# Where twelve weight sums run, when four prologue steps come, and one load that no longer waits: a Fourier filter followed by a gated MLP on one core

## The chip, the core and the metric

The kernel runs on one core of a Trainium2 chip. A core has TensorE (PE, matrix products, with its weight loads shown as PEld), VectorE (DVE), ScalarE (ACT), GpSimd (POOL) and SyncE (SP, which here only issues transfers). Each engine executes its own instructions in order; semaphores tie the engines together. Transfers issued by SP and ACT go to two queues of their own, those issued by POOL to a third. The metric is the device time of one execution in microseconds (us), the median of several.

## The reference

```python
def _attn_ref(x, filt_r, filt_i):               # x: (8, 3008, 256)
    X = np.fft.rfft(x, axis=1)
    Y = X * (filt_r + 1j * filt_i)[None, :, :]  # one complex filter, 1505 x 256
    return np.fft.irfft(Y, n=x.shape[1], axis=1).astype(np.float32)

def _moe_ref(x, w_in, w_out):                   # x: (24064, 256), w_in: 256 x 2048
    h = x @ w_in
    return ((h - np.tanh(h)) @ w_out).astype(np.float32)   # w_out: 2048 x 256
```

The second function takes the output of the first, its eight sequences laid one after the other. The weights arrive as 64-bit floats and are turned into 32-bit floats by integer operations on VectorE.

## The kernel before

**The two halves.** A sequence of 3008 is split as 64 times 47. "There" and "back" (the transforms of length 64 and 47, as products with constant matrices) turn a sequence into its spectrum and out again, with a multiplication by the filter between them. The back half ends in tiles `ut` of tokens; each group of up to four residues (256 or 224 tokens a column block) goes through the up product (256 to 2048), the shrink `h - tanh(h)`, and the down product (2048 to 256). There are 48 groups (8 sequences, 6 groups each); a group is worked in four units, and the running number of a unit is `U` (0 to 191). In unit `U` the program writes out the up product of `U`, the shrink of `U - 1` and the down product of `U - 2`.

**Products with seven instead of eight blocks.** From `U = 4` on, up and down are done with a Strassen-Winograd scheme: seven block products (`up` L564, `down` L707) instead of eight. It needs sums of the weight blocks, made once by `sums(u)` (L220): four additions of 128x256 for each of the eight weight quarters, 0 to 3 of `w_in` (tile `wu`), 4 to 7 of `w_out` (tile `wd`). It also needs sums of the tokens (`tu`) and of the shrunk values (`t`), made by `combine` (L557) on VectorE as long as weights are pending, on GpSimd later. One sum is written over a plain block, so `sums(u)` may come only after the last plain use of that quarter (`up_plain` L636, `down_plain` L788, used for `U` under 4).

**The prologue.** Sequence 0 has nothing to hide behind. It is filtered in seven slots `g` (0 to 6): `across` (transposes), `forth` (products and L377, L378), `filtered` (L389 to L401, on VectorE, with one addition, L398, on GpSimd for the slots 0 to 4), and `back0` (L1039, products L1048 and L1050, copies L1053 on ScalarE, stores to `ct2` L1054). A slot's way back is written out one slot later, so that its products follow those of the next slot's way there. The filter tiles are loaded by `filters_of` (L1021 to L1032), from slot 2 on by SP. The last slot needs one filter row that is turned round, with its sign changed: `turned_rows` (L488) loads it into `neg`, in its second step multiplies it by -1 on VectorE (L501), stores it as `less` (L502) and copies it from there into `filt` (L492), from which SP loads the last slot's tile (L1028) and seven further pieces (L1031). The two stores and the copy are issued by POOL, and the copy waits for the store's landing.

At the end of the prologue the first token tile `e2` is read back from `ct2` (`rest`, L1034, twice: first slots 0 to 4, then 5 and 6). Meanwhile TensorE runs four steps for sequence 1 (L1136) and 14 filler products (`warmer`, L999).

**Weights.** Sixteen pieces of weights are converted. The last eleven are taken by the generator `weights` (L238): it issues the loads (L169) on POOL, and each call of `next` gives one step. Its argument `after` names the quarters whose sums follow the conversion of a piece. Inside a unit, `e()` takes up to three steps and `t(k)` two of them, five times a unit each.

**What fills the gaps.** Between the blocks of a unit `t(k)` places steps of the transforms for later sequences: the first products of sequence 1 (`first`, L266, products L295, copies L297) are placed at the positions in `due`, in units of `5 U + k`.

**Order.** Everything here is in the order in which it is written; no planner moves instructions. An instruction late on VectorE therefore delays all that is behind it there. PSUM tiles of the main part have one buffer each: a product that reuses `x`, `y`, `z` or `t` waits until the last reader has taken the old contents out (for the `z` bank that is L618 or L634, for `y` L601, for `x` L626; the token products `pu`, L537, and the first products L295 share the banks `t` and `y`).

Of the kernel before, what the change touches and what calls it, by code (L numbers as in the profile page):

```python
# [9 lines left out]
F32 = mybir.dt.float32  # L10
# [17 lines left out]
NX = NH // XH  # L28
# [10 lines left out]
LEAD = 34  # L39
# [72 lines left out]
def kernel(  # L112
# [10 lines left out]
    V, G, ACT = nc.vector, nc.gpsimd, nc.scalar  # L123
# [14 lines left out]
    cst = ctx.enter_context(tc.tile_pool(name="cst", bufs=1))  # L138
# [10 lines left out]
    def extent(g):  # L149

        n = SLOTS[g][1] * NH
        return (n, DM) if g < len(SLOTS) - 1 else (2 * n, DM // 2)
# [67 lines left out]
    def sums(u):  # L220

        w = (wu if u < 4 else wd)[:, :, 256 * (u % 4):256 * (u % 4) + 256]
        by = G if 4 <= u < 7 else V
        by.tensor_add(w[:, 4], w[:, 6], w[:, 3])
        yield
        for to, one_in, less in ((5, 4, 0), (2, 1, 5), (6, 0, 6)):
            by.tensor_sub(w[:, to], w[:, one_in], w[:, less])
            yield

    def begun(tiles, job, queue=nc.sync):  # L230
# [150 lines left out]
    def filtered(g, xy, ft, by, by2, pool=None):  # L381

        n, w = extent(g)
        ab = xy.rearrange("p (x v) c -> p x v c", v=2)
        ft = ft[0:n, :, 0:w]
        fv = ft.rearrange("p (x v) c -> p x v c", v=2)
        nn = (tr.tile([128, 4, DM], F32, tag="nn", bufs=1, name="nn") if pool is None else
              pool.tile([KM, 4, DM], F32, tag="nn", bufs=3, name="nn"))[0:n, :, 0:w]
        by.tensor_mul(nn.rearrange("p (x v) c -> p x v c", v=2), ab,  # L389
                      fv[:, :, 0:1].to_broadcast([n, 2, 2, w]))  # L390
        yield nn
        if pool is not None:
            fi = ft[:, 1:4:2]
            V.tensor_mul(xy[:, 1:3], xy[:, 1:3], fi)
            V.tensor_sub(nn[:, 0:4:3], nn[:, 0:4:3], xy[:, 1:3])
            V.tensor_mul(xy[:, 0:4:3], xy[:, 0:4:3], fi)
            yield
            by2.tensor_add(nn[:, 1:3], nn[:, 1:3], xy[:, 0:4:3])  # L398
            yield
            V.tensor_add(xy[:, 0:2], nn[:, 0:2], nn[:, 2:4])  # L400
            V.tensor_sub(xy[:, 2:4], nn[:, 0:2], nn[:, 2:4])  # L401
            yield
            return
        by.tensor_mul(ab, ab, fv[:, :, 1:2].to_broadcast([n, 2, 2, w]))
        yield
        by2.tensor_sub(nn[:, 0:4:3], nn[:, 0:4:3], xy[:, 1:3])
        by2.tensor_add(nn[:, 1:3], nn[:, 1:3], xy[:, 0:4:3])
        yield
        V.tensor_add(xy[:, 0:2], nn[:, 0:2], nn[:, 2:4])
        V.tensor_sub(xy[:, 2:4], nn[:, 0:2], nn[:, 2:4])  # L410
        yield
# [97 lines left out]
    def load_e2(b, c, parts=None, tiles=None):  # L509

        e2, gt = tiles or (tr.tile([128, CH, DM], F32, tag="e2", bufs=2, name="e2"),
                           tr.tile([128, CH, 64], F32, tag="gt", bufs=2, name="gt"))
        if tiles is None:
            nc.sync.dma_start(gt, (pairs_d if b else g_d)[:, CH * 64 * c:CH * 64 * (c + 1)])
        if parts is None:
            nc.sync.dma_start(e2, dram(ct2[b], CH * c * DM,
                                       [[(PAD if b else NH) * DM, 128], [1, CH * DM]]))
        return e2, gt
# [5 lines left out]
    e2s, uts = {}, {}  # L524
# [38 lines left out]
    hs, gs = {}, {}  # L563

    def up(U, d, e, s, t):

        i, u = divmod(U, 4)
# [382 lines left out]
    with tc.tile_pool(name="tr", bufs=2) as tr, tc.manual_schedule():  # L950
# [16 lines left out]
        with tc.tile_pool(name="pro", bufs=1) as pro, \  # L967
# [55 lines left out]
            def filters_of(g):  # L1023

                t, queue = filt[g % 3], G if g < 2 else nc.sync
                if g == len(SLOTS) - 1:
                    V.memset(t[0:1, 2:4], 0.0)
                    queue.dma_start(t[NH:KL, 2:4], dram(filt_d, (turned * 8 + 5) * DM,  # L1028
                                                        [[8 * DM, NH], [2 * DM, 2], [1, DM]]))
                for v, row, n, src in filter_rows(g):  # L1030
                    queue.dma_start(t[row:row + n, v], src)  # L1031
                return t  # L1032
# [73 lines left out]
            fts = {0: filters_of(0)}  # L1106
# [42 lines left out]
            last_g = len(SLOTS) - 1  # L1149
# [19 lines left out]
            for g in range(last_g + 1):  # L1169
                if g + 2 <= last_g:  # L1170
                    fts[g + 2] = filters_of(g + 2)
                    a2[g + 2] = across(g + 2)
                if g == 3:
                    e2s[0] = load_e2(0, 0, ())
                    ones_1 = first1(load_x(big([128, 8, DM], F32, "x1"), 1, 0, 8))
                if g == last_g - 1:
                    under(fts[last_g])
                    convert(3)
                    way_back()
                if g < last_g:  # L1180
                    there[g + 1] = there0(g + 1)
                next(there[g][0])
                if g < last_g - 1:
                    convert(3)
                xy = there.pop(g)[1]
                chain = filtered(g, xy, fts.pop(g), V, V if g >= last_g - 1 else G, pro)
                nn = next(chain)
                for _ in range(2):
                    next(chain)
                if g in summed:  # L1190
                    next(chain)
                ended.append((back, (0, g, xy, z0, (ACT, nc.sync))) if g in summed else (back0, (g, nn)))
                if g not in (0, last_g - 1):
                    way_back()
                if g == 1:
                    next(turning)
                if g == 2:
                    ahead = [begun(tiles1, job, queue=G) for job in jobs[5:7]]
            rest(0, SG * (last_g - 1), [nc.sync])
            way_back()  # L1200
            rest(SG * (last_g - 1), NA - SG * (last_g - 1), [nc.sync])
            there_yet = cst.tile([128, 1], F32, name="there_yet")
            G.tensor_copy(there_yet, e2s[0][0][:, 0, 0:1])
            fs = first(2, z2, [(1, c) for c in range(2, NX)])
            next(fs)
            convert(100)
            late = weights(tiles1, jobs[5:], G, ahead, 3,
                           after={6: (0,), 8: (1,), 10: (2, 3, 4, 5, 6)})
            next(late)
            for _ in ones_1:  # L1210
                pass
# [2 lines left out]
        with tc.tile_pool(name="dn", bufs=2) as dn, \  # L1214
# [60 lines left out]
                                 start=True, stop=True)  # L1275
            for _ in range(4):
                next(late)
            due = [7 + (LEAD - 7) * k / (NX + 4) for k in range(NX + 4)]
            plan = []
            kinds = {(2, 0): "there", (1, 3): "back"}  # L1280
            kinds.update({at: "filter" for at in FILTERED})
# [2 lines left out]
            for U in range(total + 2):  # L1284
                i, u = divmod(U, 4)
                if U == 6:
                    assert not pending
                    late = sums(7)
                if U == 3:
                    G.dma_start(mats[:, 0:10 * PAD], wide_d[0:KM])  # L1290
                if U < total:
# [18 lines left out]
                def converting(n):  # L1310

                    for _ in range(n):
                        if next(late, pending) is pending:
                            pending.clear()
# [5 lines left out]
                def e():  # L1320

                    next(dw, None)
                    converting(3 if U > 1 else 1)

                def s():

# [85 lines left out]
```

## Time and profile before

| | us |
|---|---|
| median of 3 executions (2583.92 to 2587.75) | 2584.98 |
| the profiled execution | 2587.2 |
| its span | 2585.3 |
| TensorE busy in it | 2556.4 (99%) |
| VectorE busy | 1821.1 (70%) |
| ScalarE busy | 1661.8 (64%) |
| GpSimd busy | 1475.9 (57%) |

The profiled execution took 2.2 us more than the median, and 1.9 us of it lie outside the span. TensorE is not idle more than 28.9 us in all. Its granted clock over the span is 0.996 of full speed. The columns of a window row are: the stretch, its length, the busy time and count of PE, PEld, DVE, ACT and POOL, then the granted clock of TensorE, the share of the transfer engines in use and GB/s. A timeline row has start, duration, engine, line, operation, output and inputs; in square brackets stands how long the engine had been idle before it and what released it. A row of the chain has start, length and the engine and line that the end of the program hung on at that time; its lengths run from one start to the next, so a row there is shorter than the pipelined duration of the same products in the timeline.

### The profile page before, as it was taken

What the parts mean: (1) busy time and instruction counts of PE and PEld (TensorE: products, weight loads), DVE (VectorE), ACT (ScalarE), POOL (GpSimd) and SP (SyncE); (2) the same over time, 40 slices, a digit from 0 to 9 for tenths busy, and PEclk for the clock granted to TensorE, in tenths of its full rate; (3) what the DMA queues carried; (4) which work ended last, traced back from release to release, by engine and by line L of the source; (5) the groups of instructions that cost most, each with busy time, mean ns of one, the idle gap of its engine ahead of it and who ended that gap; (6) DMA issues with size and microseconds to landing.
All of it is one profiled execution on the core that took longest, in us unless ns stands there. A gap on an engine that the chain in (4) does not pass through costs nothing.

```text
span 2585.3 us, 43442 instructions
## 1 busy us (share of the span) xinstructions
PE 2556.4 (99%) x16596; PEld 2176.2 (84%) x16596; DVE 1821.1 (70%) x2222; ACT 1661.8 (64%) x2482; POOL 1475.9 (57%) x1138
## 2 busy tenths in 40 slices
PE   8999999999999999999999999999999999999998
PEld 7668888888898888988888888888889888898887
DVE  6877776877567775778657876588766877555555
ACT  4556666666666666666666666666666666666665
POOL 5366665666556665665646565466655766545552
PEclk9999999999999999999999999999999999999999
DMA  8863216441434324333243432444231322110110
GB/s 222 265 178 105 70 30 123 111 102 44 95 75 106 86 59 93 84 88 94 50 101 80 102 78 51 94 96 103 66 71 42 93 66 43 33 32 18 25 21 18
DMA packets 345333, 214.30 MB, mean 83 GB/s; under 512 B 245337, under 2 KB 316535, under 8 KB 341469
## 3 DMA queue, kind: packets, MB, share of 16 engines
q1 hardware_dynamic: 321551, 170.82, 28.7%
q10 hardware_dynamic: 12142, 23.60, 3.0%
q0 software_dynamic: 11424, 17.03, 2.4%
q8 instruction: 132, 2.16, 0.3%
q14 instruction: 84, 0.69, 0.1%
HBM read 130.72 MB, written 83.39 MB: 83 GB/s over the span
## 4 chain that ended last, share of the span: by engine, by line
PE 96%; DVE 1%; DMA 1%; issue 0%; ACT 0%; POOL 0%; ACTq 0%; DVEq 0%; POOLq 0%
PE o L748 43%; PE x L578 25%; PE z L578 12%; PE y L578 6%; PE pm L360 2%; PE pu L537 2%; PE pf L307 1%; PE o L803 1%; PE pf L295 1%; PE o L648 0%; DMA fh<-f 0%; PE pm L362 0%; DMA neg<-in_filt_i_dram 0%; DMA mats_sb<-mats 0%; PE x L648 0%
## 5 line engine op out<-in xcount | busy, mean ns | idle before, releaser
L748 PE MATMUL o<-t,wd 128*128 128x256 f32 (+1 forms) x3008 | 762.1, 376 | 0.0
L558 POOL TENSOR_TENSOR t<-h 128x512 f32<-128x512 f32 (+1 forms) x186 | 305.3, 1641 | 740.1 <-DVE h L700 718.7
L700 DVE TENSOR_TENSOR h<-h,y 128x1024 f32<-128x1024 f32 (+1 forms) x384 | 577.3, 1503 | 165.4 <-ACT y L696 161.8
L748 PEld LDWEIGHTS o<-t,wd 128*128 128x128 f32 x3008 | 569.2, 190 | 82.4 <-POOL o L776 15.1
L578 PE MATMUL x<-tu,wu 128*128 128x256 f32 (+1 forms) x2256 | 579.0, 379 | 0.0
L748 PE MATMUL o<-h,wd 128*128 128x256 f32 (+1 forms) x2256 | 572.8, 376 | 1.8 <-DVE h L700 1.8
L584 ACT COPY s<-x 128x512 f32<-128x512 f32 (+1 forms) x188 | 108.8, 579 | 601.3 <-PE x L578 556.5
L748 PEld LDWEIGHTS o<-h,wd 128*128 128x128 f32 x2256 | 426.0, 190 | 71.4 <-issue 20.5
L578 PEld LDWEIGHTS x<-tu,wu 128*128 128x128 f32 x2256 | 420.9, 190 | 66.8 <-issue 13.5
L693 ACT ACTIVATE y<-y 128x1024 f32<-128x1024 f32 (+1 forms) x384 | 399.3, 1040 | 12.1
L696 ACT ACTIVATE y<-y 128x1024 f32<-128x1024 f32 (+1 forms) x384 | 399.8, 1041 | 4.6
L690 ACT ACTIVATE y<-h 128x1024 f32<-128x1024 f32 (+1 forms) x384 | 400.3, 1042 | 3.5 <-DVE h L626 1.7
L559 POOL TENSOR_TENSOR t<-h,t 128x512 f32<-128x512 f32 (+1 forms) x186 | 306.2, 1646 | 14.6
L560 POOL TENSOR_TENSOR t<-h 128x512 f32<-128x512 f32 (+1 forms) x186 | 288.4, 1551 | 0.0
L561 POOL TENSOR_TENSOR t<-h,t 128x512 f32<-128x512 f32 (+1 forms) x186 | 287.4, 1545 | 0.0
L584 ACT COPY u<-x 128x512 f32<-128x512 f32 (+1 forms) x376 | 213.7, 568 | 56.6 <-PE x L578 53.9
L626 DVE COPY h<-x 128x512 f32<-128x512 f32 (+1 forms) x188 | 127.9, 680 | 136.7 <-PE x L578 136.4
L578 PE MATMUL z<-ut,wu 128*128 128x256 f32 (+1 forms) x752 | 191.1, 377 | 3.6 <-DVE h L618 3.6
L578 PE MATMUL x<-ut,wu 128*128 128x256 f32 (+1 forms) x752 | 190.7, 376 | 0.0
L578 PE MATMUL y<-ut,wu 128*128 128x256 f32 (+1 forms) x752 | 190.0, 375 | 0.0
L578 PE MATMUL z<-tu,wu 128*128 128x256 f32 (+1 forms) x752 | 190.0, 375 | 0.0
L601 DVE TENSOR_TENSOR h<-y,s 128x512 f32<-128x512 f32 (+1 forms) x188 | 126.6, 673 | 69.6 <-PE y L578 62.3
(197 smaller groups left out, 2758.0 us busy)
## 6 DMA issues: line engine op xcount, KB each, us to landing
ft<-filt SPq DMA_DIRECT2D x28, 1024.0 KB
ct<-nn SPq DMA_DIRECT2D x56, 512.0 KB
e<-ct SPq DMA_DIRECT2D x47, 512.0 KB
a<-ct SPq DMA_DIRECT2D x112, 192.0 KB
out_dram<-ot SPq DMA_DIRECT2D x1248, 16.0 KB
x_sb<-in_x_dram SPq DMA_DIRECT2D x74, 256.0 KB
ct<-a ACTq DMA_DIRECT2D x62, 256.0 KB
gt<-g_pairs SPq DMA_DIRECT2D x42, 128.0 KB
```

Source lines behind the costliest of these rows:

```text
L558: by.tensor_sub(t[0], b[0][1], b[0][0])
L559: by.tensor_sub(t[1], b[1][1], t[0])
L560: by.tensor_sub(t[2], b[1][1], b[0][1])
L561: by.tensor_sub(t[3], b[1][0], t[1])
L578: nc.tensor.matmul(bank[:, k], wu[:, q - 1, (2 * u + k) * 128:(2 * u + k + 1) * 128], rhs[q - 1], start=(first and k == 0), stop=True, ski ...
L584: ACT.copy(t, X)
L626: V.tensor_copy(h[:, 2, :, 0:w], X)
L690: ACT.activation(y[k], ht[k], AF.Arctan, scale=TURN)
L693: ACT.activation(y[k], y[k], AF.Tanh, scale=BEND)
L696: ACT.activation(y[k], y[k], AF.Square, scale=SCALE, accum_out=y_sums[:, 2 * U + k // 2:2 * U + k // 2 + 1])
L700: V.tensor_mul(ht[k], ht[k], y[k])
L748: nc.tensor.matmul(product(q), wd[:, q - 1, (2 * u + k) * 128: (2 * u + k + 1) * 128], rhs[q - 1][:, k], start=(u == 0 and k == 0 and q == ...
```

## The change

- `sums` is done on VectorE for all eight quarters; before, the quarters 4, 5 and 6 were done on GpSimd.
- The generator takes only the quarters 2 and 4 behind the last piece of weights, and the quarters 3, 5, 6 and 7 are done from `U = 6` on (before: 2, 3, 4, 5 and 6 behind the last piece and 7 from `U = 6`). From `U = 6` on `e()` takes no step any more, so two steps follow each `t(k)`: ten in a unit.
- In slot 0 of the prologue the addition L398 is done by VectorE.
- The second step of the turned row (L501, L502, L492) is written behind slot 2, ahead of two loads of weights; before, it stood behind slot 1.
- The copy `there_yet` (L1203) is gone; POOL's loads of weights behind it no longer wait for the tile `e2`.
- `due` starts at position 4 instead of 7 and ends at the same place. One step of the first products moves into unit 0 for that, one other moves from right behind the token products of unit 3 to the end of that unit, and a later one (unit 8) falls away.

```diff
     def sums(u):
         w = (wu if u < 4 else wd)[:, :, 256 * (u % 4):256 * (u % 4) + 256]
-        by = G if 4 <= u < 7 else V
-        by.tensor_add(w[:, 4], w[:, 6], w[:, 3])
+        V.tensor_add(w[:, 4], w[:, 6], w[:, 3])
         yield
         for to, one_in, less in ((5, 4, 0), (2, 1, 5), (6, 0, 6)):
-            by.tensor_sub(w[:, to], w[:, one_in], w[:, less])
+            V.tensor_sub(w[:, to], w[:, one_in], w[:, less])
             yield
...
-                chain = filtered(g, xy, fts.pop(g), V, V if g >= last_g - 1 else G, pro)
+                chain = filtered(g, xy, fts.pop(g), V, V if g in (0, last_g - 1, last_g) else G, pro)
...
-                if g == 1:
+                if g == 2:
                     next(turning)
-                if g == 2:
                     ahead = [begun(tiles1, job, queue=G) for job in jobs[5:7]]
...
-            there_yet = cst.tile([128, 1], F32, name="there_yet")
-            G.tensor_copy(there_yet, e2s[0][0][:, 0, 0:1])
...
             late = weights(tiles1, jobs[5:], G, ahead, 3,
-                           after={6: (0,), 8: (1,), 10: (2, 3, 4, 5, 6)})
+                           after={6: (0,), 8: (1,), 10: (2, 4)})
...
-            due = [7 + (LEAD - 7) * k / (NX + 4) for k in range(NX + 4)]
+            due = [4 + (LEAD - 4) * k / (NX + 4) for k in range(NX + 4)]
...
                 if U == 6:
                     assert not pending
-                    late = sums(7)
+                    late = (None for u in (3, 5, 6, 7) for _ in sums(u))
...
                 def e():
                     next(dw, None)
-                    converting(3 if U > 1 else 1)
+                    converting((U < 6) * (3 if U > 1 else 1))
```

## The prediction, written before the changed kernel had run

> **What bounds the kernel now.** I read the page's first part, then the windows, then who waited for whom on TensorE, then the chain in order of time. The page says that TensorE is the bound and how little is left there.
>
> ```profile
> span 2585.3 us, 43442 instructions
> PE 2556.4 (99%) x16596; PEld 2176.2 (84%) x16596; DVE 1821.1 (70%) x2222; ACT 1661.8 (64%) x2482; POOL 1475.9 (57%) x1138
> ```
>
> 28.9 us are idle, and no matmul is removed. So the change can only win idle time and time at a slowed clock. The windows show where TensorE idles once the token products run:
>
> ```profile
> 128.00:137.00 9.00, 6.88 (x18) 4.24 (x18) 7.23 (x16) 3.62 (x7) 5.09 (x7) 0.81 0.85 220
> 137.00:157.00 20.00, 15.04 (x53) 9.98 (x52) 19.66 (x26) 8.40 (x13) 18.98 (x23) 0.95 0.77 213
> 187.00:205.00 18.00, 18.00 (x143) 15.66 (x142) 16.04 (x16) 12.27 (x18) 15.44 (x10) 1.00 0.22 50
> ```
>
> From 137 to 157 VectorE (third figure behind the length) is busy 19.66 of 20 us and GpSimd 18.98, TensorE 15.04: there VectorE is the bound. From 187 to 205 TensorE is full and VectorE has 2 us left. The waits of TensorE between 84 and 260 us, beside one in the chain:
>
> ```profile
> PE z L578 <- DVE h L618: 3.6, 1, 3.6
> PE pf L295 <- DVE h L601: 1.4, 1, 1.4
> ```
>
> ```profile
> 120.70 1.73 PE pf L295 x8
> ...
> 123.93 1.50 PE o L648 x4
> ...
> 128.25 2.10 issue
> 130.35 3.00 PE pf L295 x8
> 133.35 2.16 PE o L648 x4
> ...
> 155.16 2.08 PE z L578 x4
> 157.24 1.53 PE x L578 x4
> 158.77 0.86 PE y L578 x4
> ```
>
> Behind the waits of 2.1 and 3.6 us the same products take longer: 3.00 and 2.16 instead of 1.73 and 1.50, then 2.08 and 1.53 instead of 0.86 each. That is 1.27 + 0.66 + 1.22 + 0.67 = 3.8 us of slowed clock (granted 0.81 over 128 to 137). With 2.1 + 1.4 + 3.6 = 7.1 us of waits, 10.9 us is the most that this stretch can give.
>
> **The sums leave GpSimd.** The rows of VectorE for 137 to 157 (first fence, window 137 to 155) beside those of the same work from 85 to 125 (second), and GpSimd's own (third; mean ns behind the busy us):
>
> ```profile
> L195 DVE TENSOR_TENSOR wd<-xy 128x256 f32<-128x256 f32 x4 | 4.7, 1206 | 0.1
> L700 DVE TENSOR_TENSOR h<-h,y 128x896 f32<-128x896 f32 x2 | 3.2, 1596 | 0.0
> L186 DVE TENSOR_SCALAR xy<-xy 128x512 int32<-128x512 int32 x2 | 1.7, 862 | 0.1
> L188 DVE SCALAR_TENSOR_TENSOR xy<-a,xy 128x512 f32<-128x512 uint32 x1 | 1.6, 1620 | 0.0
> ```
>
> ```profile
> L700 DVE TENSOR_TENSOR h<-h,y 128x896 f32<-128x896 f32 x4 | 4.3, 1084 | 0.0
> L186 DVE TENSOR_SCALAR xy<-xy 128x512 int32<-128x512 int32 x8 | 4.0, 506 | 0.3
> L195 DVE TENSOR_TENSOR wd<-xy 128x256 f32<-128x256 f32 x10 | 3.9, 422 | 0.2
> L188 DVE SCALAR_TENSOR_TENSOR xy<-a,xy 128x512 f32<-128x512 uint32 x4 | 2.8, 692 | 0.1
> ```
>
> ```profile
> L227 POOL TENSOR_TENSOR wd<-wd 128x256 f32<-128x256 f32 x9 | 7.1, 791 | 1.0 <-PE o L803 0.6
> L1253 POOL DMA_DIRECT2D filt<-in_filt_r_dram x4 | 2.5, 619 | 0.0
> ```
>
> While GpSimd adds (12 additions, about 0.79 each), VectorE's own work is slower: 4 x 0.784 + 2 x 0.512 + 2 x 0.356 + 0.928 = 5.8 us in these four groups. Up to some 1.5 us of it may belong to GpSimd's transfer issues (0.6 to 1.3 us each), which stay, so 4.3 to 5.8 us go. Behind the last piece VectorE does eight additions as before (2 and 4 in place of 2 and 3), so nothing is added there. VectorE gains another 1 us because the step L295 no longer stands between the token products and the next up product: it need not wait for the banks `t` and `y` (the 2.1 us), and VectorE's wait for that product goes. Together VectorE reaches L618 5.3 to 7 us sooner, while TensorE without any wait would want it about 9 us sooner (the 10.9 less the slowed products behind it). The rest, 2 to 3.7, would remain as a wait; smaller groups that I left out (L177, L180, L224, each 0.8 to 1 us there) give up to 1.3 back. I take 1.7 us as the remainder: **9.2 us won**, ends 5 and 10.9. The step of L295 that moves into unit 0 (1.73) is paid back where one falls away in unit 8; TensorE is full at both places, so the sum is nil. If its inputs are not there by 91 us, it costs what they are late; they are issued before 82.5, so I take nothing.
>
> **The same additions on VectorE later.** Quarters 3, 5, 6 and 7 take 16 additions in units 6 and 7, 12 more than before. VectorE's row for such an addition is 0.42 us (L195 above), so 5 us. Those of quarters 3 and 5 fit: 3 stands where 7 stood, and 5 (1.7 us) falls into idle time of 1.17 and 1.01 before L618 and L626. Those of 6 and 7 do not:
>
> ```profile
> 183.46 0.69 DVE L618 TENSOR_TENSOR h<-z,u 128x512 f32<-128x512 f32 x1 [1.17 <-ACT u L584]
> 185.16 0.69 DVE L626 COPY h<-x 128x512 f32<-128x512 f32 x1 [1.01 <-PE x L578]
> 186.90 1.22 DVE L450 TENSOR_TENSOR nn<-xy,ft 128x1024 f32<-128x1024 f32 x1
> 187.07 2.19 POOL L558 TENSOR_TENSOR t<-h 128x512 f32<-128x512 f32 x1 [6.56 <-DVE h L700]
> 188.63 1.71 DVE L450 TENSOR_TENSOR nn<-xy,ft 128x1024 f32<-128x1024 f32 x1
> 195.57 0.69 DVE L544 TENSOR_TENSOR ut<-pu,odd 128x512 f32<-128x512 f32 x1 [0.80 <-ACT odd L541]
> 196.78 0.68 DVE L618 TENSOR_TENSOR h<-z,u 128x512 f32<-128x512 f32 x1
> 199.19 1.03 PE L578 MATMUL z<-ut,wu 128*128 128x256 f32 x4
> ```
>
> All eight stand ahead of the L618 at 196.78, whose end (197.46) TensorE needs at 199.19: slack 1.73, and 0.80 idle before L544, 2.5 us. The eight need 3.4 us alone. Beside GpSimd's additions, which run from 187 to 196, the L450 takes 1.71 instead of 1.22; if each pair of additions lost as much, 2 us more. The wait is then 0.9 to 2.9 us; nearest to the row of L450, but with the last pair free of GpSimd, I take **1.6 us lost**. What waits behind it (L626, L700, then GpSimd's `t`) has 4 us of VectorE idle before the next L618, and I cost it at nothing.
>
> **Prologue.** In slot 0, L398 goes from GpSimd to VectorE (0.69 as its neighbours). L501 goes a slot later.
>
> ```profile
> 32.62 0.94 DVE L177 TENSOR_SCALAR top<-top 128x512 f32<-128x512 f32 x1
> ...
> 38.37 1.05 DVE L501 TENSOR_SCALAR neg<-neg 24x256 f32<-24x256 f32 x1 [0.44 <-DMA neg<-in_filt_i_dram]
> ...
> 40.88 1.09 PE L372 MATMUL pb<-a,mats_sb 120*120 120x256 f32 x4 [2.55 <-DVE xy L378]
> ...
> 46.21 0.68 POOL L492 DMA_DIRECT2D filt<-less x1 [4.93 <-DMA less<-neg]
> ...
> 82.39 0.18 POOL L1203 COPY there_yet<-e 128x1 f32<-128x1 f32 x1 [12.74 <-DMA f<-f_both]
> ```
>
> ```profile
> 50.13 0.49 DVE top L177
> ...
> 77.36 6.04 PE warm L999 x28
> ```
>
> VectorE saves the wait 0.44 and L501's 1.05 (a tiny operation, long beside GpSimd's L398), and about 0.5 at L177 when GpSimd's addition in slot 0 is gone; it pays 0.69. So the products at 40.88 start about 1.3 us sooner, and their wait of 2.55 becomes 1.3. In this trace the wait of 1.4 us was not followed by slowed products and that of 2.1 was; so the four slowed pairs behind 40.88 should go as well, another 1 to 1.7. VectorE's L177 at 50.13 hung on that chain, so it comes up to 3 us sooner. L501 costs in slot 2 what it takes there, at most its 1.05.
>
> How much reaches the end of the prologue? The fillers end at 83.40; the last load of `e2` had landed by 82.39, so 1 us of slack lies in it. Without L1203, two loads of 512 KB that stood behind it leave POOL about 13 us sooner, beside that chain of stores and loads. I charge 0.5 us, ends 0 and all of the prologue's gain. On POOL, L502 now comes behind the second pair of stores (about 47 us) and L492 waits some 5 us for it, with two weight loads and L398 of slot 3 behind; SP's L1028 and all behind it follow. L398 late by some 3 us delays only the way back of slot 3, whose products have the whole of slot 4 before the end needs them; if SP's pieces for slot 6 come too late instead, VectorE waits there, and the lower end of 0 covers it. The prologue therefore gives **2.2 us**, ends 0 and 3.
>
> **Sum.** 9.2 + 2.2 - 1.6 = 9.8 us. The profiled execution, 2587.2, becomes 2577.4; it stood 2.2 over the median, so against 2584.98 I predict **2575.2 us**.
>
> **Rivals.**
> 1. *All at its best*: 10.9 + 3.0 - 0.9 = 13.0, 2572.0. For it speaks that the groups left out also get faster; against it that GpSimd's transfer issues stay. Chance 0.12.
> 2. *The prologue gives nothing* since the end waits for `e2` behind the two early loads: 9.2 - 1.6 = 7.6, 2577.4. Chance 0.15.
> 3. *The stretch gives its lower end*, 5, since VectorE stays the bound with GpSimd's issues still beside it, the prologue nothing, and unit 7 costs 2.9: 2.1 won, 2582.9. VectorE's 19.66 of 20 speaks for it. Chance 0.14.
> 4. *Slower: the additions of quarters 6 and 7 each stand behind a whole addition of GpSimd*. Price: 8 x (2.19 + 0.42) less 2.5 of slack, 18.4 us at the L618 of unit 7, against 11.4 won: 7.0 lost, 2592.0. It decides from 1.3 us of waiting for each addition. For it speaks that L195 averaged 1.206 us beside such additions; against it that L450 lost only 0.5, and that GpSimd adds just four times from 187 to 196. Chance 0.09. [...]
>
> My forecast has 0.50. A measurement of this kernel can tell about 0.2% (5.2 us) from no change. So faster is 0.50 + 0.12 + 0.15 = 0.77, within it 0.14, slower 0.09. The range 2571 to 2583 holds all but rival 4 and the spread at its edges. The forecast's own range is 2572.5 to 2578.5.
>
> **What would show it.** In the trace after: no wait at L295 behind the token products of unit 3, and no slowed products after it; L195 and L188 of the last pieces near 0.42 and 0.69 us; the wait for L618 in unit 5 under 2 us; a new wait of 0.9 to 2.9 us for L618 in unit 7; L501 off the chain, and the fillers' end about 2 us sooner. The forecast is wrong if the fillers' end is followed by a wait for `e2`, if SP's piece loads for slot 6 come so late that L389 there waits for them, or if the additions of quarters 6 and 7 take a microsecond each.

## The result, and the profile after

| | median (runs) | lowest to highest |
|---|---|---|
| before, beside it | 2588.34 us (20) | 2583.92 to 2591.72 |
| after | 2580.84 us (20) | 2579.68 to 2584.1 |

The ratio is 0.9973, with a 95% interval of 0.9966 to 0.9979: 7.0 us faster, between 5.4 and 8.8. The profiled execution took 2579.82 us, 7.4 less than the one of before. Lines of the changed kernel have numbers one lower than before from L224 to L1200 or so, and four lower behind that.

The first lines of the page after:

```profile
span 2578.0 us, 43442 instructions
PE 2553.1 (99%) x16596; PEld 2173.1 (84%) x16596; DVE 1818.7 (71%) x2235; ACT 1661.7 (64%) x2482; POOL 1465.8 (57%) x1124
```

The windows of the changed kernel, with the columns as before:

```profile
128.00:137.00 9.00, 8.36 (x29) 5.34 (x29) 8.34 (x19) 5.43 (x11) 7.10 (x8) 1.00 0.83 205
137.00:157.00 20.00, 19.41 (x72) 13.27 (x71) 15.77 (x29) 13.57 (x20) 11.76 (x13) 1.00 1.06 277
187.00:205.00 18.00, 17.03 (x133) 14.75 (x134) 14.40 (x17) 10.18 (x16) 11.77 (x8) 1.00 0.32 104
```

From 137 to 157 TensorE is busy for 19.41 of 20 us where it was 15.04, VectorE has 4 us free, and the clock from 128 to 137 is full. From 187 to 205 TensorE, which was full, has lost 1 us. What TensorE waits for between 84 and 260 us:

```profile
PE pu L536 <- DVE h L600: 0.8, 1, 0.8
PE y L577 <- ACT a L296: 0.6, 1, 0.6
PE x L577 <- DVE h L625: 0.6, 1, 0.6
PE z L577 <- DVE h L633: 0.4, 1, 0.4
PE z L577 <- DVE h L617: 0.4, 1, 0.4
```

The waits of 2.1, 1.4 and 3.6 us are gone; 0.6 and 0.6 (at 135.8 and 149.7) are left in that stretch. The other three lie from 183 to 194, in the units 6 and 7. VectorE's groups by shape from 128 to 146:

```profile
...
L195 DVE TENSOR_TENSOR wd<-xy 128x256 f32<-128x256 f32 x6 | 2.4, 421 | 0.1
L186 DVE TENSOR_SCALAR xy<-xy 128x512 int32<-128x512 int32 x3 | 1.9, 642 | 0.1
...
L188 DVE SCALAR_TENSOR_TENSOR xy<-ft,xy 128x512 f32<-128x512 uint32 x2 | 1.4, 693 | 0.1
```

421 and 693 ns are those operations with no addition of GpSimd beside them; from 128 to 146 it only issues transfers.

To see where the time went, four marks in the trace are enough: the start of the last way back in the prologue (L419 of slot 6), of the first token products (L536), and of the `pm` products L359 on `a` and on `xy`, which every kernel here runs. In the changed kernel, as in slot2_on_v and early_slot2 below, four of the first 64 token products start 0.6 to 0.7 us ahead of the others (here at 82.67); the mark is that of the other 60. From the last mark to the end the spans differ by less than 0.9 us in all kernels here.

| profiled execution | L419, slot 6 | L536 | L536 to L359 on `a` | from there to L359 on `xy` |
|---|---|---|---|---|
| before | 72.82 | 83.51 | 89.83 | 51.85 |
| after | 71.77 | 83.26 | 82.09 | 52.66 |

With `due` from 4, one step of L294 (1.73 us) lies in the first of these stretches that before lies in the second. So the first won 89.83 - 82.09 + 1.73 = 9.5 us, the second lost 52.66 - 51.85 + 1.73 = 2.5, and the prologue gave 0.25. The sum is 7.2, and the spans differ by 7.3.

### The profile page after: what moved, and what is told of

It is laid out like the page before. It is cut to its first block, busy times and chain, and to the rows that moved or that the text cites. A ratio compares the mean times of both kernels' runs of the same rounds, so it can differ in the third digit from the quotient of the medians.

```text
span 2578.0 us, 43442 instructions
## 1 busy us (share of the span) xinstructions
PE 2553.1 (99%) x16596; PEld 2173.1 (84%) x16596; DVE 1818.7 (71%) x2235; ACT 1661.7 (64%) x2482; POOL 1465.8 (57%) x1124
## 4 chain that ended last, share of the span: by engine, by line
PE 94%; DVE 2%; DMA 2%; ACT 1%; issue 1%; POOL 0%; ACTq 0%; SPq 0%; POOLq 0%; DVEq 0%
PE o L747 43%; PE x L577 25%; PE z L577 12%; PE y L577 6%; PE pm L359 2%; PE pu L536 2%; PE pf L306 1%; DMA ct<-a 1%; DMA x<-in_x_dram 0%; DMA ct<-e 0%; PE pm L361 0%; PE pf L294 0%; DVE h L699 0%; PE o L802 0%; DVE wd L226 0%
## 5 line engine op out<-in xcount | busy, mean ns | idle before, releaser
L577 PE MATMUL x<-tu,wu 128*128 128x256 f32 (+1 forms) x2256 | 579.0, 379 | 0.0
L577 PEld LDWEIGHTS x<-tu,wu 128*128 128x128 f32 x2256 | 420.9, 190 | 66.8 <-issue 13.5
L577 PE MATMUL y<-ut,wu 128*128 128x256 f32 (+1 forms) x752 | 190.1, 375 | 0.6 <-ACT a L296 0.6
L577 PE MATMUL x<-ut,wu 128*128 128x256 f32 (+1 forms) x752 | 190.1, 375 | 0.6 <-DVE h L625 0.6
L577 PE MATMUL z<-ut,wu 128*128 128x256 f32 (+1 forms) x752 | 190.2, 375 | 0.4 <-DVE h L617 0.4
L577 PE MATMUL z<-tu,wu 128*128 128x256 f32 (+1 forms) x752 | 190.1, 375 | 0.4 <-DVE h L633 0.4
```

What stands on the lines that cost most here:

```text
L577: nc.tensor.matmul(bank[:, k], wu[:, q - 1, (2 * u + k) * 128:(2 * u + k + 1) * 128], rhs[q - 1], start=(first and k == 0), stop=True, ski ...
```

## The experiments

Medians stand beside runs of the kernel before on the same chip, whose medians are 2587.66 to 2588.25. The first four kernels of the table ran on one chip, the next four on a second, the next three on a third and early_slot2 on a fourth, so kernels of different groups are better compared by the ratio. The marks are those of one profiled execution each.

| kernel | median us (range, runs) | ratio to before, 95% | L419 | L536 | to `a` | to `xy` |
|---|---|---|---|---|---|---|
| sums_in_place | 2580.61 (2579.39 to 2581.74, 11) | 0.9972 (0.9963 to 0.9981) | 74.62 | 85.31 | 81.56 | 51.84 |
| main_only | 2583.66 (2579.61 to 2588.67, 11) | 0.9982 (0.9973 to 0.9991) | 73.89 | 84.58 | 88.89 | 52.65 |
| prologue_only | 2588.08 (2586.77 to 2592.02, 11) | 1.0004 (0.9995 to 1.0013) | 76.84 | 87.48 | 90.95 | 51.85 |
| early_56 | 2580.55 (2577.86 to 2582.25, 7) | 0.9972 (0.9961 to 0.9983) | 77.04 | 87.68 | 82.90 | 50.12 |
| turn_back | 2583.45 (2582.14 to 2585.03, 11) | 0.9979 (0.9970 to 0.9988) | 75.13 | 86.78 | 84.19 | 52.65 |
| gate_back | 2582.07 (2580.25 to 2584.71, 11) | 0.9977 (0.9968 to 0.9986) | 75.27 | 85.91 | 83.13 | 52.66 |
| due_back | 2583.9 (2580.15 to 2586.08, 11) | 0.9985 (0.9976 to 0.9994) | 72.61 | 83.33 | 81.66 | 54.39 |
| slot0_in_place | 2580.61 (2579.31 to 2581.88, 6) | 0.9971 (0.9959 to 0.9983) | 73.34 | 84.03 | 83.37 | 51.85 |
| slot2_on_v | 2578.85 (2577.68 to 2580.72, 5) | 0.9964 (0.9951 to 0.9978) | 70.15 | 82.30 | 82.66 | 52.66 |
| early_slot1_turn | 2580.96 (2580.18 to 2586.14, 11) | 0.9977 (0.9968 to 0.9986) | 73.41 | 85.32 | 83.92 | 50.12 |
| early_all_v | 2579.27 (2578.56 to 2581.71, 6) | 0.9967 (0.9955 to 0.9979) | 73.71 | 84.35 | 83.03 | 50.12 |
| early_slot2 | 2578.34 (2577.73 to 2580.07, 5) | 0.9965 (0.9951 to 0.9978) | 69.50 | 82.29 | 84.02 | 50.12 |

### One part at a time

**sums_in_place**: the kernel before, with all sums on VectorE at their old places, and nothing else.

```diff
-        by = G if 4 <= u < 7 else V
-        by.tensor_add(w[:, 4], w[:, 6], w[:, 3])
+        V.tensor_add(w[:, 4], w[:, 6], w[:, 3])
...
-            by.tensor_sub(w[:, to], w[:, one_in], w[:, less])
+            V.tensor_sub(w[:, to], w[:, one_in], w[:, less])
```

> The kernel before with the sums of quarters 4, 5 and 6 on VectorE and nothing else: same place in the order, same steps, old prologue. Theory A (GpSimd's additions lengthen VectorE's neighbouring operations): L188, L195 and L186 of the last two pieces fall back to about 0.69, 0.42 and 0.5 us, VectorE reaches the L618 of unit 5 some 4 to 6 us sooner, the wait of 3.6 us there goes; the twelve additions (5 us) then stand behind that L618, and delay L626, L634 and L601 of units 5 and 6 by up to 5 us. Net 1 to 4 us faster than before. The wait of 2.1 us behind the token products of unit 3 stays. Theory B (VectorE is just full there, GpSimd's additions cost it nothing): the durations stay, and 12 x 0.42 = 5 us come on top: 3 to 5 us slower.

**main_only**: the change without its three edits in the prologue (L398 of slot 0, the change of sign, `there_yet`).

> The changed kernel with the prologue of before (L398 of slot 0 on GpSimd, the change of sign behind slot 1, the copy there_yet kept). Theory A (the prologue's part gives next to nothing, 0.25 us at the first token products): 6.5 to 7.5 us faster than before, like the whole change. Rival (the prologue's part helps the units by its early weight loads, or hurts them): off from the whole change by 2 us or more.

**prologue_only**: the kernel before with these three edits alone.

> The kernel before with the three edits of the prologue alone. Theory A: VectorE runs about 3 us ahead at the L177 near 47 us, gives 2 of it back by the L389 of slot 6, and the rest at the stores and loads of the first token tile beside the two early weight loads; the first token products start 0 to 0.5 us sooner, and the time is 0 to 0.5 us under before. As predicted before the result: 2.2 us faster. If the early loads take more from the later units: slower by up to 1 us.

**early_56**: the changed kernel with the sums of quarters 5 and 6 at the front again.

```diff
-                           after={6: (0,), 8: (1,), 10: (2, 4)})
+                           after={6: (0,), 8: (1,), 10: (2, 4, 5, 6)})
...
-                    late = (None for u in (3, 5, 6, 7) for _ in sums(u))
+                    late = (None for u in (3, 7) for _ in sums(u))
```

> The changed kernel with quarters 5 and 6 behind the last piece of weights too (2, 4, 5, 6), so that units 6 and 7 have eight additions (3 and 7) in place of 16. Theory A (the additions of 6 and 7 beside GpSimd's combination cost TensorE some 2.5 us in units 6 and 7): those waits go, up to 0.8 us comes back at the x bank of unit 5, so 1.5 to 2.5 us faster than the changed kernel, 8.5 to 9.5 under before. Rival (units 6 and 7 lose for another reason, the step of the first products or the GpSimd issues): same as the changed kernel, 7 under before, or less if unit 5 takes the additions badly.

Measured: the sums alone give the whole gain (0.9972 against 0.9973), the prologue's three edits alone give none (1.0004), and the new places and due times without the prologue's edits are worse than the sums alone by the median (2583.66 against 2580.61; the intervals overlap). So the other edits together bring nothing. Of these four only prologue_only's time came out as expected. sums_in_place is 7.4 us faster, where 1 to 4 were expected: theory A's shorter operations are there, but the twelve additions, done from 149.6 to 157.0 at about 0.42 us each, hold up nothing; the only wait of TensorE listed from 84 to 260 us is one of 2.2 at L294. main_only is 4.3 us faster than before instead of 6.5 to 7.5. The execution of main_only that was profiled took 2587.62 us and shows a wait that no other one has, among TensorE's waits from 84 to 178 us:

```profile
PE pf L294 <- ACT xy L175: 3.4, 1, 3.4
```

There the step of L294 stands behind ScalarE's conversion of a piece of weights in unit 1 (at 108 us). No other profile shows it. Its runs lie between 2579.6 and 2588.7; that this wait comes and goes between them would explain it, but only this one was profiled.

The units 6 and 7 are settled by early_56. VectorE's sums in the changed kernel, from 170 to 222 us by shape:

```profile
L226 DVE TENSOR_TENSOR wd<-wd 128x256 f32<-128x256 f32 x9 | 6.1, 703 | 0.1
L223 DVE TENSOR_TENSOR wd<-wd 128x256 f32<-128x256 f32 x3 | 2.3, 764 | 0.0
```

and in early_56:

```profile
L226 DVE TENSOR_TENSOR wd<-wd 128x256 f32<-128x256 f32 x3 | 1.2, 420 | 0.0
L223 DVE TENSOR_TENSOR wd<-wd 128x256 f32<-128x256 f32 x1 | 0.4, 379 | 0.0
```

The twelve additions of `wd` (quarters 5, 6 and 7) take 8.4 us, 3.4 more than at 0.42 each; the four of early_56 (quarter 7) take 1.6. From L359 on `a` to L359 on `xy` early_56 needs 50.12 us, which is before's 51.85 less the step of 1.73: nothing is lost there. So the loss of 2.5 us comes from having the eight additions of quarters 5 and 6 here, and no part of it is the earlier steps of L294. How it comes about, in the timeline of the changed kernel (VectorE and GpSimd in unit 6):

```profile
179.08 2.18 POOL L557 TENSOR_TENSOR t<-h 128x512 f32<-128x512 f32 x1 [6.52 <-DVE h L699]
180.04 1.50 DVE L223 TENSOR_TENSOR wd<-wd 128x256 f32<-128x256 f32 x1
181.34 1.34 POOL L558 TENSOR_TENSOR t<-h,t 128x512 f32<-128x512 f32 x1
181.58 1.38 DVE L226 TENSOR_TENSOR wd<-wd 128x256 f32<-128x256 f32 x1
182.64 1.45 POOL L559 TENSOR_TENSOR t<-h 128x512 f32<-128x512 f32 x1
...
184.05 2.25 POOL L560 TENSOR_TENSOR t<-h,t 128x512 f32<-128x512 f32 x1
185.09 1.83 DVE L226 TENSOR_TENSOR wd<-wd 128x256 f32<-128x256 f32 x2
```

Two additions that VectorE starts while GpSimd adds end 0.28 us behind GpSimd's: 181.54 behind 181.26, 182.96 behind 182.68. They stand for what is left of GpSimd's instruction, not for a share of it. The four additions of quarter 6 (from 180.04 on) take 4.71 us in this way, those of quarter 5, before GpSimd starts, 1.55. The median of early_56 is only 0.3 us below the changed kernel's all the same, where 1.5 to 2.5 were expected. In its profiled execution the two quarters cost 0.8 in the stretch before (82.90 against 82.09), and the prologue ended 4.4 later, since TensorE's clock stood at half for longer there (13.7 us against 3.4, below); how much of that is in every run, one profile can't say.

### Why the prologue gave nothing

Four kernels ask which edit takes back VectorE's head start.

**turn_back**: the changed kernel with the change of sign behind slot 1 again (`next(turning)` under `if g == 1`).

> The changed kernel with the change of sign put back behind slot 1; everything else as changed. Theory T (the later change of sign takes back what the early sum wins: its loads reach the filter late, so the 512 KB issues, the change of sign's own transfers and an addition all stand together on GpSimd in slots 2 and 3, and SyncE's L1027 issues at 57 instead of 54): about 2578.5 us, 2 to 2.5 below the changed kernel's 2580.8; L1027 issues near 54, L186 of VectorE no longer takes over 2 us near 53, the first token products start before 82. Theory L (the missing gain of the prologue goes to the two 512 KB loads that start beside the transfers of e2): 2580.8, as the changed kernel within 0.7, the first token products at 83 to 85 as before. Theory N (nothing in the prologue is worth anything, its end is set by something that none of the three edits touches): 2580.8 as well, and then the run with the gate put back shows the same.

**gate_back**: the changed kernel with `there_yet` again.

> The changed kernel with the gate L1200 of before put back: GpSimd again copies one element of e2 before it issues the two 512 KB loads and the weights behind them. Theory L (early loads hold up the transfers of e2): about 2578.5 us, 2 below the changed kernel. Theory T: no gain from this, 2580.8 within 0.7. Theory D (filter steps spread from 4 instead of 7 need the weights earlier, so that a filter step waits behind ScalarE's L175 where the loads were held back, as the 3.4 us of L294 in the profile of the kernel with the sums, their places and the due times alone): about 2583.5, as that kernel's 2583.7, with single runs spread from 2580 to 2588 and a wait of 2 to 4 us before L294 in the units 0 to 2.

**due_back**: the changed kernel with `due` from 7 again.

> The changed kernel with the filter steps spread from 7 again instead of 4. If the earlier spread is worth nothing where the loads are early: 2580.8 within 0.7; from the first token products to the first product of the main stage (134.75 us in the changed kernel) it takes 133.4 to 134.8. If the spread from 4 costs something of its own (a filter step that is squeezed in before its input, 0.5 to 1.5 us): 2579.5 to 2580.3. If it is what the place of the sums of quarters 5 to 7 needs (fewer filter steps in the units 6 and 7, so the additions there have room): about 2582.5, with waits over 1 us before L577 or L536 between 180 and 200.

**slot0_in_place**: sums_in_place with L398 of slot 0 on VectorE.

> The kernel before with all sums of the weights on VectorE at their old places, and with the filter's sum of slot 0 on VectorE; gate, change of sign, due times and places as before. Theory T (the early sum is worth 2 to 3 us where the change of sign stays where it was): 2578.0 to 2578.8, against 2580.6 of the kernel that has the sums on VectorE alone; L177 of slot 2 starts near 47 instead of 50, the first token products start near 82. Theory L says the same of this kernel, since its loads are gated as before. Theory N: 2580.6 within 0.7, and the first token products at 83.5 to 85.5.

Measured: 2583.45, 2582.07, 2583.9 and 2580.61. Each of three edits undone alone (the change of sign, the gate, the due times) makes the changed kernel slower by its median, by 1.2 to 3.1 us, though each interval of the ratio overlaps the changed kernel's. Slot 0's sum alone, put into sums_in_place, leaves the median where it was (2580.61), and its token products start at 84.03, within the 83.51 to 85.31 of the three executions with the old prologue: no part of theory T's gain appears there. Theory T falls: with the change of sign early, the waits before L1049 are at most 1.6 us, but TensorE runs at half its clock from 61 to 68 us, L419 of slot 6 starts at 75.13, the token products wait 1.07 for the reload of `e2`, and 1.0 for L296 at 131 us. Theory L falls: with the gate the time is 1.2 us longer, not 2 shorter (theory D's wait for L175 isn't in its profile either; it is 1.3 us for L296 before L577). due_back did not decide: its runs spread over 6 us, and the one profiled (2580.68) was among its fastest. It does confirm one number: from `a` to `xy` it takes 54.39, which is 51.85 and the 2.5 of the additions.

The traces point at GpSimd's queue. The timeline of the changed kernel, slots 3 and 4:

```profile
50.50 0.69 DVE L395 TENSOR_TENSOR xy<-xy,filt 120x512 f32<-120x512 f32 x1
...
52.68 0.68 POOL L491 DMA_DIRECT2D filt<-less  x1 [4.92 <-DMA less<-neg]
...
53.35 0.74 POOL L169 DMA_DIRECT2D ft<-in_moe_w_in_dram  x1
53.74 2.67 DVE L186 TENSOR_SCALAR low<-top 128x512 int32<-128x512 int32 x1
54.09 0.74 POOL L169 DMA_DIRECT2D ft<-in_moe_w_out_dram  x1
54.83 1.29 POOL L397 TENSOR_TENSOR nn<-nn,xy 120x512 f32<-120x512 f32 x1
...
56.17 1.21 PE L1049 MATMUL pe<-nn,mats_sb 120*120 120x256 f32 x2 [4.02 <-POOL nn L397]
...
57.17 1.06 PE L1047 MATMUL pe<-nn,mats_sb 120*120 120x256 f32 x2
58.02 1.06 PE L1049 MATMUL pe<-nn,mats_sb 120*120 120x256 f32 x2
```

VectorE has everything for the sum L397 of slot 3 ready at 51.2. GpSimd stands at L491, which waits 4.92 us for the store of the turned row, then issues it and two loads, and adds at 54.83, where the kernel before added at 54.45. TensorE waits 4.02 us and then runs at half its clock (1.06 instead of 0.59 for two products). VectorE's L186 ends 0.29 us behind GpSimd's addition, 2.67 us for what takes 0.43 when nothing holds it. The head start ends there.

Four more of the kernels here have the same prologue up to there, and each shows the wait before these products: 4.4 us in gate_back, 4.1 in due_back, 4.07 in early_56, 3.7 in prologue_only. In the other nine no wait for such a sum is over 1.8. In the changed kernel, prologue_only and early_56 an operation of VectorE is held until just behind GpSimd's addition, but not the same one: L186 for 2.67 and 2.33 us, L188 for 2.32. The timeline of early_56:

```profile
55.81 2.32 DVE L188 SCALAR_TENSOR_TENSOR low<-raw,low 128x512 f32<-128x512 uint32 x1
56.28 1.29 POOL L397 TENSOR_TENSOR nn<-nn,xy 120x512 f32<-120x512 f32 x1
...
57.63 1.21 PE L1049 MATMUL pe<-nn,mats_sb 120*120 120x256 f32 x2 [4.07 <-POOL nn L397]
```

What differs is how long the clock then stays low. The same microsecond in the changed kernel (first) and in early_56:

```profile
60.00:61.00 1.00, 1.00 (x6) 0.87 (x5) 0.92 (x2) 0.00 (x0) 0.50 (x1) 1.00 0.61 170
```

```profile
60.00:61.00 1.00, 1.00 (x4) 0.79 (x3) 0.97 (x2) 0.38 (x1) 0.00 (x0) 0.50 1.00 389
```

By windows of a microsecond, TensorE's clock stands at half for 3.4 us before L419 of slot 6 in the changed kernel and in due_back, for 10.2 in gate_back and for 13.7 in early_56, and L419 follows: 71.77, 72.61, 75.27, 77.04. If half of that time counts as lost (an estimate), the four come to 70.1 to 70.9, and the three kernels with the old prologue, which have 6.8 us of it each, to 69.4 to 71.2. So the head start is gone in all four, and most of the 5.3 us between executions of one program is the clock.

**slot2_on_v**: the changed kernel with one more sum on VectorE.

```diff
-                chain = filtered(g, xy, fts.pop(g), V, V if g in (0, last_g - 1, last_g) else G, pro)
+                chain = filtered(g, xy, fts.pop(g), V, V if g in (0, 2, last_g - 1, last_g) else G, pro)
```

> The changed kernel with one more of the filter's sums (L397) on VectorE, that of slot 2. Theory Q (the head start of VectorE in the prologue is lost in GpSimd's queue: in the new order the sum of slot 2 stands behind the transfer L491, which waits 4.9 us there for the change of sign's own round trip, and behind two 512 KB issues, so TensorE waits 4.0 us before L1049 and then runs for 3 to 7 us at half the clock): the wait before L1049 near 54 falls from 4.0 us to under 1, the first back product of slot 6 (L419) starts at 68.5 to 70.5 instead of 71.8 to 77.0, the run takes 2577.5 to 2579, 2 to 3 us below the changed kernel's 2580.8. Rival R (the end of the prologue is set by the transfers of slot 6's row, which come later with the later change of sign): a wait of 2 to 4 us before L371 or L419 takes its place and the time is 2580.8 within 0.7.

The expectation named the wrong slot: the sum behind L491 is that of slot 3, not of slot 2. The edit still does what it was made for, by another path: without slot 2's addition GpSimd stores the turned row 1.25 us sooner (45.96 for 47.21), and the landing comes quicker too, so that L491 starts 3.55 us sooner. Why it lands quicker isn't shown. The timeline of slot2_on_v there:

```profile
49.13 0.68 POOL L491 DMA_DIRECT2D filt<-less  x1 [2.62 <-DMA less<-neg]
...
51.28 1.29 POOL L397 TENSOR_TENSOR nn<-nn,xy 120x512 f32<-120x512 f32 x1
52.49 1.60 POOL L1053 DMA_DIRECT2D ct<-e  x2
...
52.63 0.69 PE L1049 MATMUL pe<-nn,mats_sb 120*120 120x256 f32 x2 [0.38 <-POOL nn L397]
...
53.52 0.43 DVE L186 TENSOR_SCALAR low<-top 128x512 int32<-128x512 int32 x1
```

The wait of 4.02 is 0.38, L186 is 0.43, the next products run at full clock, L419 of slot 6 starts at 70.15, and the median is 2578.85, 2.0 us below the changed kernel. Theory Q's wait goes and its forecast of the time is met; that it was met with the wrong slot named is luck. The clock stands at half for 3.4 us here too, so by the estimate above L419 comes to 68.4 (in early_slot2, below, to 67.8), some 2 us sooner than in the four kernels with the wait. The interval of the ratio overlaps most of the changed kernel's (0.9966 to 0.9979), so 2.0 us in the whole time are not sure; four of the five runs lie below all 20 of the changed kernel.

**early_slot1_turn** (early_56 with the change of sign behind slot 1, and the sums of slots 0 and 1 on VectorE) and **early_all_v** (early_56 with every sum of the filter on VectorE):

> The changed kernel with three edits: the sums of quarters 5 and 6 stand at the front again (two quarters only in the units 6 and 7: 3 and 7), the change of sign is back behind slot 1, and the filter's sum of slot 1 is on VectorE beside that of slot 0, so that no sum of the filter stands behind L491 on GpSimd. Theory Q: the waits before L1049 fall to 1.6 us at most, slot 6's row is there in time, and with the 2.5 us of the units 6 and 7 won back as in the kernel with two quarters there, the run takes 2576 to 2578.5. Rival R: L371 or L536 waits 1 to 2 us for a transfer, as 1.3 and 1.1 us in the kernel with the change of sign put back alone, and the run takes 2579 to 2581.

> The changed kernel with the sums of quarters 5 and 6 at the front again and the filter's sum of every slot on VectorE; the change of sign behind slot 2 as changed. Theory Q: no wait of TensorE for a sum on GpSimd is left; VectorE has 4 sums of 0.69 us more than the changed kernel, and so the run takes 2576.5 to 2578.5. If VectorE's 2.8 us are themselves on the path (rival V): waits before L1047, L371 or L419 for VectorE grow by 2 us or more and the run takes 2579.5 to 2581. Rival R: as for the kernel with slot 2 alone, a wait of 2 to 4 us for a transfer of slot 6's row, 2580 to 2582.

early_slot1_turn took 2580.96, as rival R said: L536 waits 1.33 us for the reload of `e2`, and TensorE runs slow from 60 to 67 us behind waits of 1.8 and 1.6. early_all_v took 2579.27, between theory Q and rival V: no wait for GpSimd is left, but one of 3.0 us before L1047 for VectorE and one of 1.9 before L371 for a transfer.

**early_slot2**: slot2_on_v and early_56 together.

> The kernel with the filter's sum of slot 2 on VectorE (2578.85 us), and beside that the sums of quarters 5 and 6 at the front again, so that the units 6 and 7 have four additions in place of eight. Theory F (each of the eight additions stands a whole GpSimd addition of the t combination, and TensorE is full without them: from the first product of the first way out to the first of the second 52.66 us with eight, 50.12 with four): 50.1 us there again, and 1.7 to 2.5 us less in all, 2576.4 to 2577.2; the wait before L1049 stays at 1.6 us or less. Rival V (VectorE has no room for the four additions in the units 1 to 3 either, so what is won in the units 6 and 7 is lost there): 2578.5 to 2580, with waits of over 1 us before L536 or L577 between 100 and 160.

By the edit there are eight additions in place of sixteen in the units 6 and 7, not four in place of eight. It took 2578.34 us, the lowest median of all, and 0.5 less than slot2_on_v where 1.7 to 2.5 were expected; beside the kernel before on their own chips the two are equal (0.9965 and 0.9964). The units 6 and 7 gave what theory F said (50.12 us), and rival V's waits of over 1 us before L536 or L577 are not there. 1.4 us were given back in the stretch before (84.02 against 82.66): TensorE stood idle for 1.46 us ahead of the first token products, and the products behind them ran at half the clock (the block of L1270 takes 3.56 us instead of 1.99). Although its slot 6 was 0.65 us ahead, its token products start at 82.29, as slot2_on_v's at 82.30.

## Why the prediction was right, and where it was off

Faster was right, and 2580.84 lies in the range of 2571 to 2583, which is wide, but not in the forecast's own of 2572.5 to 2578.5. Nearest in its gain was rival 2 (7.6 us, chance 0.15), by other terms than it named: 9.5 won, 2.5 lost, 0.25 from the prologue. The gain was 7.0 to 7.5 us instead of 9.8; the rest of the distance to 2575.2 is that the kernel before measured 2588.34 beside it, 3.4 above the median that the forecast started from.

1. **The stretch from 128 to 157**: 9.2 predicted, 9.5 by the marks. VectorE's pieces came to 0.42 and 0.69 us, no wait and no slow product follows unit 3's token products, and what remains is 1.2 us of waits where 1.7 was taken. sums_in_place shows that moving the twelve additions off GpSimd is enough for 8.3 of it (89.83 to 81.56), in an execution where the wait of 2.2 us at L294 stays and no slow products follow it; slot0_in_place, with the same wait and slow products behind it, has 6.5. The step of 1.73 us moved at no cost, as said.
2. **The units 6 and 7**: 1.6 lost predicted, 2.5 measured, within its ends (0.9 to 2.9). The term was undersized because of quarter 6: its additions meet GpSimd's four from 179 to 186 in unit 6 and take 4.71 us instead of 1.7, where the prediction added 2 us for all of quarters 6 and 7. Quarter 5 does run in idle time, as said. The waits are spread (0.4 before L633's bank in unit 6, 0.8 at L536, 0.4 in unit 7) instead of one wait at L617. The argument from L450's 1.71 for 1.22 took a partial overlap for a slowdown: L450 starts 0.63 us before GpSimd's addition ends (189.26) and ends 1.08 behind it, so it too stands for what is left. What rival 4 named, additions that stand while GpSimd adds, is what the rows show (1.50 and 1.38 us in place of 0.42), but its price was not: those additions stand for what is left of GpSimd's, which cost 3.4 us over all twelve, and 18.4 was out of reach.
3. **The prologue**: 2.2 predicted, 0.25 in the two traces and nothing in prologue_only (1.0004). This is the step that failed. Its first half was right: VectorE's L177 comes 3.1 us sooner, as the chain of the changed kernel has it, L500 takes 0.28 us and is off the chain, and the slow products behind 40.88 are gone.

```profile
46.99 0.48 DVE top L177
```

   Wrong was the sentence that L398 of slot 3, three microseconds late behind L492, "delays only the way back of slot 3". TensorE executes its products in the order written, and behind those of slot 3's way back stand those of slot 4's way back and of slot 6's way there (at 65.22; slot 5's, at 49.83, stands ahead): it waited 4.02 us with nothing else to do. And VectorE, which needs nothing from that sum, was held in L186. Undoing the later change of sign did not bring the 2.2 us either (turn_back, 2583.45): there the wait of 4 us is gone, but the clock stands at half for 6.8 us. What brought some 2 us at L419 is slot2_on_v, which shortens the wait in GpSimd's queue. The other changed prologues without that wait (turn_back, slot0_in_place, early_slot1_turn, early_all_v) come to 69.9 to 71.7 by the same estimate, each with waits of TensorE of 1.6 and 1.8 us, or of 3.0 and 1.9. So this wait is what the step costs in the changed kernel; that the head start reaches the end once it is gone isn't shown.
4. **The end of the prologue.** The chain of the changed kernel there:

```profile
72.88 6.36 DMA ct<-e
...
80.45 2.67 DMA e<-ct
83.12 0.14 issue
83.26 0.75 PE pu L536 x35
```

   Most of the token products follow the reload of `e2`, not the fillers, which end 1.0 us sooner than before instead of about 2: the wait that rival 2 named, and that the prediction gave as a sign of being wrong, is there. In the changed kernel it costs 0.8 us (11.49 from L419 to L536; 10.6 to 10.7 in the nine kernels without such a wait), and in slot2_on_v and early_slot2 it sets 82.3 as the end whatever slot 6 does. The 0.5 us charged for it were about right; none of the five kernels with the gate has the wait, and five of the nine without it have, so the early loads may well be its cause; gate_back, which has the gate and no wait, is not faster for it.

Open is why single runs of main_only and due_back spread over 6 to 9 us, since no kernel was profiled in two of its runs (spells of half clock, as in the prologue, could do it), and what of turn_back's 2.6 us comes from where. In the prologue L419 of slot 6 lies between 69.5 and 77.0 in the profiled executions, so differences of a microsecond between two of them prove little; the readings above rest on waits that one kernel has and the other has not.

## What to carry to other kernels

Work that two engines can share is moved off the one that here held up the other's operations, and placed where that other is idle: twelve additions on the other engine gave 7 us, and eight additions put beside the first engine's own later ones cost 2.5. Before a step is moved in an engine's program, read what stands behind it in that queue: a transfer that waits for another transfer's landing (L491, 4.92 us) held back a sum here that has nothing to do with it. A head start in one engine is worth what the next queue lets through, so follow it to the end of the stage before counting it.

## What the runs showed of the hardware

**The same wait slows the clock in one execution and not in another.** TensorE's timeline of sums_in_place and of slot0_in_place, at the same step, and the window behind it:

```profile
132.39 1.97 PE L294 MATMUL pf<-x_sb,f 128*128 128x256 f32 x8 [2.21 <-issue]
```

```profile
134.00:136.00 2.00, 2.00 (x7) 1.12 (x6) 1.93 (x6) 0.71 (x2) 0.61 (x1) 1.00 0.76 164
```

```profile
131.51 2.60 PE L294 MATMUL pf<-x_sb,f 128*128 128x256 f32 x8 [2.19 <-issue]
```

```profile
134.00:136.00 2.00, 2.00 (x4) 0.91 (x3) 1.65 (x5) 0.62 (x2) 0.06 (x1) 0.50 0.69 175
```

After 2.21 us idle the granted clock is 1.00, after 2.19 it is 0.50; the first stretch is 1.8 us longer for it (83.37 against 81.56). In the prologue of these traces a slow spell lasts 3.4 or 6.8 us, and the wait ahead of it doesn't say which: behind the same wait of about 4 us it is 3.4 in the changed kernel and due_back and 6.8 in gate_back and early_56, and behind prologue_only's 3.7 none follows at once. In early_slot2 one began at 83.6, behind waits of 1.46 us (to 81.58) and 0.38 us (to 82.29). What decides whether a spell follows a wait, and which of the two lengths it has, isn't shown.

**A VectorE operation with one input took six times its length beside GpSimd.** L186 took 2.67 us instead of 0.43, from 53.74 until just behind GpSimd's L397 (54.83 to 56.12). It was already standing while GpSimd issued the load at 54.09, but in slot2_on_v it took 0.43 while GpSimd issued the stores L1053. In early_56, at the same step, it took 0.63 and ended 0.23 us behind the first of the two issues L169, and the next operation (L188, rows above) was held until behind the addition. In the changed kernel an L186 at 137.76 took 1.08 and ended 0.24 us behind an issue L1253 (137.34 to 138.60). So by these rows an addition can hold it, and an issue can, but not every issue does; what decides isn't shown. VectorE's waits in the changed kernel's trace (0 to 84 us) do not list it: only the length of the operation shows it.
